# Weights converted ahead of a mask, a sigmoid under its own table, a last product in two banks, and outputs from another queue

## The chip, the cores and the metric

The kernel runs on one core of one Trainium2 chip. The core has a matrix engine (TensorE, PE in the profile), a vector engine (VectorE, DVE), an activation engine (ScalarE, ACT), GpSimd (POOL) and a sync engine (SP) that mainly issues transfers. Each engine takes its own instructions strictly in order, and the engines wait for one another through semaphores. Matmuls write to PSUM, which is divided into banks; DVE and ACT read the results from there. The metric is the device time of one execution in microseconds, lower is better; the profile shows one execution by itself.

## The reference

The first block is a gated linear recurrence over 768 tokens, for 4 batches and 8 heads of 48 channels. The second is a feed-forward block with a gate, of 384 to 1536 to 384 channels, over all 3072 tokens.

```python
f = 1.0 / (1.0 + np.exp(-f_logit))
for t in range(S):
    state = f[:, :, t, :, None] * state + k[:, :, t] (outer) v[:, :, t]
    y[:, :, t] = q[:, :, t] @ state
x = y.transpose(0, 2, 1, 3).reshape(B * S, H * D)
g = x @ w_gate
out = (g * sigmoid(g) * (x @ w_val)) @ w_out
```

Here "(outer)" stands for the outer product that the reference writes as an einsum. The three weight matrices come in 64-bit floats, everything else in 32-bit floats.

## The kernel before, in words

**Tiling.** The sequence is cut into six chunks of 128 tokens. A unit is one batch's part of one chunk, so chunk 0 holds units 0 to 3, chunk 1 units 4 to 7, and so on. The recurrence inside a chunk is done with products: `attention(u)` applies a sigmoid to the gates, multiplies them up in scans over time (`tails` at L549, `head` at L562), scales k and q with the results (`kT` at L559, `qT` at L568), multiplies the two into scores (`sc`, L586), masks the scores to the causal part (`A`, L596) and multiplies with v (`y`, L639, or L614 and L618). ACT then copies y into `xT` (L654), from which the feed-forward products of the chunk are made. The function is a generator: each `yield` ends a step, and the callers decide which other work goes between steps.

**Loads.** `load(u, what)` issues the transfers of f, k, q and v of a unit from SP. In chunks 0 and 1 f, k and q go to two rotating buffers each (`raw`), so a load has to wait until PE has transposed the unit two before.

**Weights.** [...]the weights come in pieces of 768 KB: `fetch` issues the transfer (L447) into one of four buffers, `sizes` has ACT make two tiles from a piece (`up` at L459, `top` at L461, each with two buffers), and `join` has DVE put them together in four kinds of steps (L467, L469, L471, L473), the last of which writes the weight. The first piece of the gate weights and the first of the value weights are converted in two halves each, so that the first product can start early; the lists `fetches`, `sizes` and `joins` hold what is still to be done, in order. A fetch has to wait until the piece four before has been read by both engines.

**Order.** The first part (chunk 0's recurrence, and the first steps of unit 4) is written out by hand around L1098 to L1157. At its end `in_order` makes PE, DVE and ACT keep the order in which the code was written. SP is not in that list, so a scheduler places its transfers. After that, `take_turns` mixes the feed-forward products of chunk 0 (`mlp_plain`: gate products at L712 with a silu on ACT at L724, value products with a multiply on DVE at L728, then the downward products at L737) with the recurrence of chunk 1, and with the rest of the weights.

**Tables.** ACT needs a table for sigmoid and another for silu, and loading one is an instruction of its own. Copies, absolute values and scalings work under either. In the first part ACT goes from silu back to the sigmoid of unit 4 (L535) and then to silu again.

**Chunks 1 to 5.** Their feed-forward block runs through `mlp_fifteen`, a scheme with fifteen block products instead of eighteen for each of the gate and the value, and then `down_seven`, seven block products instead of eight. Products go to PSUM banks from three pools: "A" (two banks), "B" (one) and "o" (two). ACT copies banks aside (`c` and `aside`, L892), and DVE adds and subtracts them (L786, L789). What DVE or the queues have to do after a product is put in `lagging` by `lag`, and written behind the next product. The outer loop takes the pieces of all chunks by due time and mixes in the recurrence of the chunk after.

**The end of a chunk.** In `down_seven`, `five` ends with the two additions for the upper output half `kept["o", 1]`, one of which reads the bank of `kept["p4"]`. `seven(0)` and `seven(1)` then make the last product, for two groups of 128 tokens. Both write the same bank, each half of it. After each, DVE adds it to `u5` into `kept["o", 0]`, and `put_out` (L997) issues the transfer of 192 KB to the output. All four output transfers of a chunk are issued from ACT's queue, except the very last of the kernel, which is issued from SP's. For chunks 1 to 4 DVE's eleven sums of tokens for the next chunk (`token_sums`, in L786 to L792) stand ahead of those two additions.

Of the kernel before, what the change touches and what calls it, by code (L numbers as in the profile page):

```python
# [12 lines left out]
AF = mybir.ActivationFunctionType  # L13
# [276 lines left out]
def short_path(ctx, tc, ident, least, judge, q, k, v, f_logit, moe_w_gate, moe_w_val, moe_w_out, out):  # L290
# [9 lines left out]
    nc = tc.nc  # L300
    B, H, S, D = q.shape
    C = 128
    NCH = S // C
    HP = H // 2
    W = 64
    DM = H * D
# [4 lines left out]
    N1 = C + 1  # L311
    NRAW = 2
# [24 lines left out]
    raw = {nm: [first_pool.tile([128, H, W], FP32, tag=f"{nm}raw{i}", name=f"{nm}raw{i}") for i in range(NRAW)]  # L337
           for nm in "qkf"}
# [23 lines left out]
    def pairs(t, off=0):  # L362
        return t[:, off:off + HP * N1].rearrange("p (a t) -> p a t", t=N1)
# [49 lines left out]
    def load(u, what="fkqv"):  # L413
        b, c = units[u]
        rows = slice(c * C, (c + 1) * C)
        for nm, src in (("f", f_logit), ("k", k), ("q", q), ("v", v)):
            if nm not in what:
                continue
            if nm == "v":
                dst = v_of(u)  # L420
            elif c < SQUARES:
                dst = raw[nm][u % NRAW]
            else:
                for n in range(4):
                    at = Q * (1 - n % 2)
                    nc.sync.dma_start(
                        out=rooms[nm][Q * n:Q * (n + 1), at:at + HP * RUN].rearrange("t (a e) -> t a e", a=HP),
                        in_=src[b, n // 2::2, rows, :].rearrange("a (t i) d -> t a (i d)", i=NI))
                continue
            nc.sync.dma_start(out=dst[:, :, 0:D], in_=src[b, :, rows, :].rearrange("h t d -> t h d"))  # L430
# [84 lines left out]
    def bank(name):  # L515
        return banks[-1].tile([128, 512], FP32, tag="a", name=name)

    def attention(u):
        b, c = units[u]
        fr, kr, qr = (raw[nm][u % NRAW] for nm in "fkq")  # L520
# [10 lines left out]
        if c >= SQUARES:  # L531
            nc.scalar.activation(squares("f"), squares("f"), AF.Sigmoid)
        else:
            p = transposed("fTp", fr)
            nc.scalar.activation(pairs(gate)[:, :, 1:N1], p, AF.Sigmoid)  # L535
        yield
        if c >= SQUARES:
            nc.vector.transpose(in_turn(pairs(gate)[:, :, 1:N1]), squares("f"))
# [145 lines left out]
    def in_order(since, engines):  # L684

        start = len(traced)
        while traced[start - 1] is not since:
            start -= 1
        for engine in engines:
            keep_order([ins for ins in traced[start:] if ins.engine == engine])  # L690
# [145 lines left out]
    def lag(f, *args):  # L836
        lagging.append(lambda: f(*args))  # L837
# [129 lines left out]
    def down_seven(c, h):  # L967

        DH = DM // 2
        s1 = [comb.tile([128, TH], FP32, tag=f"hs{j}", name=f"hs{j}") for j in range(NP)]
        b11, b12 = w_out[:, 0:NP, 0:DH], w_out[:, 0:NP, DH:DM]
        b21, b22 = w_out[:, NP:NF, 0:DH], w_out[:, NP:NF, DH:DM]
        kept = {}
        order = [*range(0, NP, 2), *range(1, NP, 2)]

        def hidden_sums(j):
            a11, a21, a12, a22 = (h[j][:, k, :] for k in range(4))
            plus(s1[j], a21, a22)  # L980
            minus(a21, a11, a21)

        def bank2(name, tag):
            pool = {"A": banks_a, "B": banks_b, "o": banks_o}[tag]
            return pool.tile([128, 512], FP32, tag=tag, name=name)[:, 0:DM].rearrange("p (n d) -> p n d", n=2)

        def add(p, lhsTs, rhs, first, part):
            for j in order[part * NP // 2:(part + 1) * NP // 2]:
                for n in range(2):
                    nc.tensor.matmul(p[:, n, :], lhsT=lhsTs[j][:, n * C:(n + 1) * C], rhs=rhs[:, j, :],  # L990
                                     start=first and j == order[0] and n == 0, stop=j == order[-1],
                                     skip_group_check=True)

        def of_h(k):
            return [h[j][:, k, :] for j in range(NP)]

        def put_out(half, n, queue):  # L997
            t0 = (2 * half + n) * S + c * C
            queue.dma_start(out=out[t0:t0 + C, :], in_=kept["o", half][:, n, :])

        def one(part):
            if part == 0:
                kept["o", 0], kept["o", 1] = out_rooms()
                kept["u"], kept["u5"] = (comb.tile([128, 2, TH], FP32, tag=t, name=t)[:, :, 0:DH]
                                         for t in ("c12", "c22"))
                kept["p"] = bank2("o11", "B")
            add(kept["p"], of_h(0), b11, True, part)
            if part:
                nc.scalar.copy(kept["u"], kept["p"])
                for j in order:  # L1010
                    lag(minus, h[j][:, 0, :], s1[j], h[j][:, 0, :])

        def two(part):
            add(kept["p"], of_h(2), b21, False, part)
            if part:
                nc.scalar.copy(kept["o", 0][:, :, 0:DH], kept["p"])
                for j in order:
                    lag(minus, h[j][:, 2, :], h[j][:, 2, :], h[j][:, 0, :])

        def three(part):  # L1020
            if part == 0:
                kept["p"] = bank2("o6", "A")
            add(kept["p"], of_h(0), down_sums[2], True, part)
            if part:
                lag(plus, kept["u"], kept["u"], kept["p"])

        def four(part):
            if part == 0:
                kept["p5"] = bank2("o5", "B")
            add(kept["p5"], s1, down_sums[1], True, part)  # L1030
            if part:
                lag(plus, kept["u5"], kept["u"], kept["p5"])

        def five(part):
            if part == 0:
                kept["p"] = bank2("o7", "o")
            add(kept["p"], of_h(1), b12, True, part)
            if part:
                lag(plus, kept["u"], kept["u"], kept["p"])
                lag(plus, kept["o", 1][:, :, DH:DM], kept["u"], kept["p5"])  # L1040
                lag(plus, kept["o", 1][:, :, 0:DH], kept["u"], kept["p4"])
                for n in range(2):
                    lag(put_out, 1, n, nc.scalar)

        def six(part):
            if part == 0:
                kept["p4"] = bank2("o4", "o")
            add(kept["p4"], of_h(3), down_sums[4], True, part)

        def seven(n):  # L1050
            if n == 0:
                kept["p"] = bank2("o3", "A")
            for j in order:
                nc.tensor.matmul(kept["p"][:, n, :], lhsT=h[j][:, 2, n * C:(n + 1) * C], rhs=b22[:, j, :],
                                 start=n == 0 and j == order[0], stop=j == order[-1], skip_group_check=True)
            lag(plus, kept["o", 0][:, n, DH:DM], kept["u5"][:, n, :], kept["p"][:, n, :])
            lag(put_out, 0, n, nc.sync if n and c == NCH - 1 else nc.scalar)

        return hidden_sums, [(DOWN / 2, lambda f=f, part=part: f(part))
                             for f in (one, six, two, three, four, five, seven) for part in range(2)]  # L1060
# [28 lines left out]
    def weights():  # L1089
        if fetches:  # L1090
            fetches.pop(0)()
        if sizes:
            sizes.pop(0)()
        if joins:
            joins.pop(0)()
# [10 lines left out]
    def run(b, *steps):  # L1106
        for s in steps:
            assert done[b] == s
            done[b] += 1
            for _ in range((3, 1, 4, 2, 3)[s]):  # L1110
                next(first[b])

    def load_ahead(u):

        if u + NRAW < B:
            load(u + NRAW, "fkq")
        load(u + 1, "v")
        fetches.pop(0)()
        if u + NRAW >= B:
            load(u + NRAW, "fkq")  # L1120

    run(0, 0, 1, 2)
# [1 line left out]
    for b in range(1, B):  # L1124
        if b == 1:
            run(1, 0)
            keep_warm(6)
        run(b, 1)
        run(b - 1, 3)
        run(b, 2)  # L1130
        load_ahead(b)
        if b + 1 < B:
            run(b + 1, 0)
        else:
            sizes.pop(0)()
        run(b - 1, 4)
    run(B - 1, 3)
    joins.pop(0)()
    run(B - 1, 4)

    hidden, last = mlp_plain(0)
    steps = attention_steps(1)
    for _ in range(2):
        sizes.pop(0)()
        joins.pop(0)()
    load(B + 1, "v")
    for _ in range(2):
        sizes.pop(0)()
    hidden[0]()
# [2 lines left out]
    joins.pop(0)()  # L1152
    hidden[1]()
    weights()
    hidden[2]()
    steps.pop(0)()
    in_order(mark, (mybir.EngineType.PE, mybir.EngineType.DVE, mybir.EngineType.Activation))  # L1157

# [135 lines left out]
```

## Time and profile before

The median of three runs is 622.11 us (620.12 to 622.82). The profiled execution has a span of 618.6 us.

| Engine | busy, us | share of the span |
|---|---|---|
| PE (matmul) | 599.7 | 97% |
| DVE | 500.3 | 81% |
| ACT | 293.5 | 47% |
| POOL | 5.0 | 1% |

By stage, from the busy times of each stretch:

| Stretch, us | what runs | PE busy | DVE busy | share of DMA engines in use |
|---|---|---|---|---|
| 0 to 31 | recurrence of chunk 0 | 24.70 of 31 | 25.81 | full |
| 31 to 62 | feed-forward of chunk 0 begins, weights arrive | 29.05 of 31 | 28.15 | full |
| 62 to 107 | its gate and value products | 45.00 of 45 | 42.58 | 0.58 |
| 148 to 245 | chunk 1 | 96.54 of 97 | 89.99 | 0.33 |
| 245 to 342 | chunk 2 | 96.14 of 97 | 80.45 | 0.28 |
| 608 to 618.6 | the last product and the outputs | 3.94 of 10.6 | 2.19 | 0.24 |

A busy PE need not be a PE at its peak, as matmuls are pipelined and their ends modelled. What counts for this change is where PE is not busy, and what ended those idle times. A weight load (PEld) runs beside the matmul ahead of it.

### The profile page before, as it was taken

What the parts mean: (1) busy time and instruction counts of PE and PEld (TensorE: products, weight loads), DVE (VectorE), ACT (ScalarE), POOL (GpSimd) and SP (SyncE); (2) the same over time, 40 slices, a digit from 0 to 9 for tenths busy, and PEclk for the clock granted to TensorE, in tenths of its full rate; (3) what the DMA queues carried; (4) which work ended last, traced back from release to release, by engine and by line L of the source; (5) the groups of instructions that cost most, each with busy time, mean ns of one, the idle gap of its engine ahead of it and who ended that gap; (6) DMA issues with size and microseconds to landing.
All of it is one profiled execution on the core that took longest, in us unless ns stands there. A gap on an engine that the chain in (4) does not pass through costs nothing.

```text
span 618.6 us, 10913 instructions
## 1 busy us (share of the span) xinstructions
PE 599.7 (97%) x4060; PEld 490.1 (79%) x4060; DVE 500.3 (81%) x961; ACT 293.5 (47%) x535; POOL 5.0 (1%) x27
## 2 busy tenths in 40 slices
PE   7898999999999999999999999999999999999995
PEld 4744545667888898888899788899888889888895
DVE  7889999878999978868897877987887985566741
ACT  2485645313875621557711557632367640366600
POOL 1000000000000000000000000000000000000000
PEclk9999999999999999999999999999999999999998
DMA  9999583005231324222224320323321300100001
GB/s 150 236 246 254 172 231 92 5 23 161 63 86 51 85 61 125 69 48 64 51 77 117 91 52 19 84 62 95 107 75 33 81 6 10 52 2 0 1 2 56
DMA packets 95678, 50.95 MB, mean 82 GB/s; under 512 B 56064, under 2 KB 89472, under 8 KB 95616
## 3 DMA queue, kind: packets, MB, share of 16 engines
q1 hardware_dynamic: 92304, 45.64, 30.5%
q10 hardware_dynamic: 3312, 4.52, 2.0%
q8 instruction: 34, 0.56, 0.4%
q14 instruction: 28, 0.23, 0.1%
HBM read 42.47 MB, written 4.72 MB: 76 GB/s over the span
## 4 chain that ended last, share of the span: by engine, by line
PE 77%; DVE 12%; ACT 4%; DMA 3%; issue 2%; SPq 1%; ACTq 0%; DVEq 0%
PE o L990 16%; PE A L887 15%; PE B L887 11%; PE o L737 5%; PE o L887 5%; PE c L887 5%; PE sc L586 4%; PE val L712 4%; PE gate L712 3%; PE y L618 2%; PE kt L590 2%; PE y L614 1%; PE dS L659 1%; DVE head L562 1%; DMA fraw<-in_f_logit_dram 1%
## 5 line engine op out<-in xcount | busy, mean ns | idle before, releaser
L887 PE MATMUL A<-xs,w_both 128*128 128x256 f32 x240 | 62.6, 383 | 3.5 <-ACT c L892 2.3
L990 PE MATMUL o<-w_out,h 128*128 128x192 f32 x360 | 62.1, 328 | 0.2 <-ACT aside L892 0.2
L990 PEld LDWEIGHTS o<-w_out,h 128*128 128x128 f32 x360 | 58.6, 190 | 0.8 <-ACT aside L892 0.4
L887 PEld LDWEIGHTS A<-xs,w_both 128*128 128x128 f32 x240 | 44.5, 190 | 12.4 <-ACT c L892 3.9
L892 ACT COPY c<-A 128x512 f32<-128x512 f32 x40 | 23.3, 583 | 65.1 <-DVE ob L786 33.9
L786 DVE TENSOR_TENSOR c<-c,aside 128x512 f32<-128x512 f32 x60 | 41.1, 686 | 14.8 <-ACT aside L892 13.8
L892 ACT COPY aside<-A 128x512 f32<-128x512 f32 x60 | 35.0, 583 | 33.0 <-PE A L887 33.0
L789 DVE TENSOR_TENSOR c<-c,aside 128x512 f32<-128x512 f32 x60 | 41.2, 687 | 7.3 <-ACT aside L892 7.3
L837 DVE TENSOR_TENSOR h<-h,c 128x256 f32<-128x256 f32 x100 | 41.2, 421 | 7.0 <-ACT h L903 6.7
L990 PE MATMUL o<-ws,h 128*128 128x192 f32 x240 | 41.7, 328 | 0.0
L887 PE MATMUL B<-xT,extra 128*128 128x256 f32 x160 | 41.4, 382 | 0.0
L887 PE MATMUL c<-xT,w_both 128*128 128x256 f32 x160 | 41.3, 381 | 0.0
L887 PE MATMUL A<-xs,extra 128*128 128x256 f32 x160 | 41.2, 380 | 0.0
L887 PE MATMUL B<-xs,w_both 128*128 128x256 f32 x160 | 41.1, 380 | 0.0
L903 ACT ACTIVATE h<-c 128x256 f32<-128x256 f32 x100 | 39.2, 415 | 3.0 <-DVE c L789 1.9
L892 ACT COPY aside<-B 128x512 f32<-128x512 f32 x60 | 34.9, 582 | 10.6 <-PE B L887 10.2
L990 PEld LDWEIGHTS o<-ws,h 128*128 128x128 f32 x240 | 39.2, 190 | 0.3 <-issue 0.2
L789 DVE TENSOR_TENSOR c<-o,c 128x512 f32<-128x512 f32 x40 | 27.5, 689 | 14.6 <-ACT h L903 9.5
L596 DVE TENSOR_TENSOR A<-sc,causal 128x512 f32<-128x512 f32 x48 | 30.6, 678 | 6.0 <-PE sc L586 6.0
L887 PEld LDWEIGHTS B<-xs,w_both 128*128 128x128 f32 x160 | 30.4, 190 | 4.1
L887 PEld LDWEIGHTS c<-xT,w_both 128*128 128x128 f32 x160 | 30.2, 190 | 4.3 <-DVE c L789 0.2
L887 PEld LDWEIGHTS A<-xs,extra 128*128 128x128 f32 x160 | 30.3, 190 | 4.1
(134 smaller groups left out, 1155.0 us busy)
## 6 DMA issues: line engine op xcount, KB each, us to landing
fsquares<-in_f_logit_dram SPq DMA_DIRECT2D x64, 96.0 KB, 2.3
ksquares<-in_k_dram SPq DMA_DIRECT2D x64, 96.0 KB, 2.3
qsquares<-in_q_dram SPq DMA_DIRECT2D x64, 96.0 KB, 2.3
v<-in_v_dram SPq DMA_DIRECT2D x24, 192.0 KB, 3.3
w<-in_moe_w_gate_dram SPq DMA_DIRECT2D x6, 768.0 KB, 6.1
w<-in_moe_w_val_dram SPq DMA_DIRECT2D x6, 768.0 KB, 5.6
w<-in_moe_w_out_dram SPq DMA_DIRECT2D x6, 768.0 KB, 5.3
out_dram<-ob ACTq DMA_DIRECT2D x23, 192.0 KB, 2.0
```

Of the source, the lines that this page charges most:

```text
L586: nc.tensor.matmul(sc[par][:, a * C:(a + 1) * C], lhsT=kT[r, a, :], rhs=qT[r, a, :], start=True, stop=True)
L590: nc.tensor.transpose(p[:, a * C:(a + 1) * C], kT[:, a, :], ident)
L596: nc.vector.tensor_tensor(A[:, par], sc[par].rearrange("p (a t) -> p a t", t=C), causal.unsqueeze(1).broadcast_to((128, HP, C)), ALU.mult)
L712: nc.tensor.matmul(p, lhsT=w[:, j, i, :], rhs=xT[c][:, i, :], start=(i == 0), stop=(i == KT - 1))
L737: nc.tensor.matmul(p, lhsT=h[n // 2][:, n % 2 * 2 + b // 2, b % 2 * C:(b % 2 + 1) * C], rhs=w_out[:, j, :], start=(n == 0), stop=(n == NF ...
L786: nc.vector.tensor_tensor(dst, a, b, ALU.add)
L789: nc.vector.tensor_tensor(dst, a, b, ALU.subtract)
L837: lagging.append(lambda: f(*args))
L887: nc.tensor.matmul(p[name][:, n, :], lhsT=weights_of[a][:, n, j, :], rhs=tokens[b], start=fresh and n == 0, stop=True, skip_group_check=True)
L892: nc.scalar.copy(t, p[name])
L903: nc.scalar.activation(dst, src[:, 0, :], AF.Silu)
L990: nc.tensor.matmul(p[:, n, :], lhsT=lhsTs[j][:, n * C:(n + 1) * C], rhs=rhs[:, j, :], start=first and j == order[0] and n == 0, stop=j == ...
```

## The change

The change has five edits, in three places.

1. **First weights before the mask.** The first half of the first gate piece is joined, and the first half of the value piece prepared, ahead of step 3 of the last unit of chunk 0, which holds its mask. The aim is that DVE does something useful while it waits for the scores.
2. **One sigmoid while its table is loaded.** A new function, `sigmoid_ahead`, applies the sigmoid to the raw gates of unit 4 before PE transposes them and before the first silu is due. After the transposition ACT only copies them. The aim is to spare the change to the sigmoid's table and back.
3. **Loads in written order.** f, k and q of unit 5 are no longer loaded from `load_ahead(3)`, but together with its v after the next weight piece has been fetched. SP joins the engines whose order is kept in this first part. For the transfers after it, the scheduler is still free: in the built program the v of unit 7 stands ahead of that weight piece.
4. **The last product in two banks.** `seven(0)` takes a bank from pool "A" and `seven(1)` one from pool "o", each as a product of its own. The bank that pool "o" gives is the one that `kept["p4"]` had.
5. **Outputs from SP's queue.** The two transfers of the lower output half are issued from SP for every chunk. The two of the upper half stay with ACT.

```diff
+    def sigmoid_ahead(u):
+        fr = raw["f"][u % NRAW]
+        nc.scalar.activation(fr, fr, AF.Sigmoid)
+        ahead.add(u)
...
-            nc.scalar.activation(pairs(gate)[:, :, 1:N1], p, AF.Sigmoid)
+            nc.scalar.activation(pairs(gate)[:, :, 1:N1], p, AF.Copy if u in ahead else AF.Sigmoid)
...
         def seven(n):
-            if n == 0:
-                kept["p"] = bank2("o3", "A")
+            p = bank2("o3", "Ao"[n])[:, n, :]
             for j in order:
-                nc.tensor.matmul(kept["p"][:, n, :], lhsT=h[j][:, 2, n * C:(n + 1) * C], rhs=b22[:, j, :],
-                                 start=n == 0 and j == order[0], stop=j == order[-1], skip_group_check=True)
-            lag(plus, kept["o", 0][:, n, DH:DM], kept["u5"][:, n, :], kept["p"][:, n, :])
-            lag(put_out, 0, n, nc.sync if n and c == NCH - 1 else nc.scalar)
+                nc.tensor.matmul(p, lhsT=h[j][:, 2, n * C:(n + 1) * C], rhs=b22[:, j, :], start=j == order[0],
+                                 stop=j == order[-1])
+            lag(plus, kept["o", 0][:, n, DH:DM], kept["u5"][:, n, :], p)
+            lag(put_out, 0, n, nc.sync)
...
-        if u + NRAW >= B:
+        if u + NRAW == B:
             load(u + NRAW, "fkq")
...
+    joins.pop(0)()
+    sizes.pop(0)()
     run(B - 1, 3)
+    sizes.pop(0)()
     joins.pop(0)()
     run(B - 1, 4)
...
-    for _ in range(2):
-        sizes.pop(0)()
-        joins.pop(0)()
-    load(B + 1, "v")
+    sigmoid_ahead(B)
+    joins.pop(0)()
     for _ in range(2):
         sizes.pop(0)()
...
     weights()
+    load(B + 1)
     hidden[2]()
     steps.pop(0)()
-    in_order(mark, (mybir.EngineType.PE, mybir.EngineType.DVE, mybir.EngineType.Activation))
+    in_order(mark, (mybir.EngineType.PE, mybir.EngineType.DVE, mybir.EngineType.Activation, mybir.EngineType.SP))
```

In the built program, three other things follow in the first part. The scores of unit 4 (`sc`) stand ahead of the third value product on PE rather than in the midst of it. On DVE, the first step (L467) of the third gate piece now stands ahead of the last step (L473) of the value piece before it, and so ahead of unit 4's scan (L549). And SP issues k, q and v of units 5 and 6 ahead of the third value piece.

More of the change, by code (lines that the diff above doesn't have):

```diff
@@ L516, in bank @@
         return banks[-1].tile([128, 512], FP32, tag="a", name=name)
+    ahead = set()
+    def sigmoid_ahead(u):
+        fr = raw["f"][u % NRAW]
+        nc.scalar.activation(fr, fr, AF.Sigmoid)
+        ahead.add(u)
     def attention(u):
```

## The prediction

> **What bounds the kernel now.** I began with the page's shares of the engines, then the waits of TensorE (PE) over the whole span, then the timeline at the places those waits name. PE is busy for 97% of the span, so the end moves only by what PE stands idle, plus what follows its last product.
>
> ```profile
> PE 599.7 (97%) x4060; PEld 490.1 (79%) x4060; DVE 500.3 (81%) x961; ACT 293.5 (47%) x535; POOL 5.0 (1%) x27
> ```
>
> PE's waits (engine, tile and line, who ended the wait, then total us, times, longest):
>
> ```profile
> PE sc L586 <- DVE qT L568: 3.3, 3, 1.8
> PE A L887 <- ACT c L892: 2.3, 4, 0.6
> ...
> PE fTp L527 <- DMA fraw<-in_f_logit_dram: 1.7, 3, 0.8
> PE gate L712 <- DVE w_both L473: 0.7, 1, 0.7
> ```
>
> Three concern the change: one wait of 1.8 us on `qT`, four of about 0.6 us on ScalarE (ACT) copies, and the first gate product's 0.7 us. From 60 to 150 us PE waits for nothing, so an early saving is carried through that stretch.
>
> The start of the first product, in the timeline (start, duration, engine, line; in brackets the idle time before it):
>
> ```profile
> 27.86 1.29 DVE L596 TENSOR_TENSOR A<-sc,causal 128x512 f32<-128x512 f32 x2 [1.25 <-PE sc L586]
> 29.07 0.35 DVE L467 TENSOR_SCALAR top<-top 128x384 f32<-128x384 f32 x1
> 29.93 0.48 ACT L654 COPY xT<-y 128x384 f32<-128x384 f32 x1 [0.83 <-PE y L639]
> 30.44 0.56 DVE L473 CUSTOM_DVE_ANT_0 w_both<-top,up 128x768 uint16<-128x768 uint16 x1
> ...
> 42.78 0.56 DVE L467 TENSOR_SCALAR top<-top 128x768 f32<-128x768 f32 x1 [1.59 <-ACT top L461]
> ```
>
> VectorE (DVE) idles 1.25 us before the mask of unit 3, then joins the first weights (L467 to L473, until 31.00); the gate starts at 31.14. At 42.78 DVE waits for ACT, which loads a table at 37.37, at 39.28 and at 42.76, 1.28 us each. The scan for unit 4 follows at 46.38, `qT` ends at 51.53, and PE's `sc` starts at 51.67 after the 1.81 us.
>
> The turn from one chunk to the next, and the end:
>
> ```profile
> 245.45 1.03 PE L887 MATMUL o<-xT,w_both 128*128 128x256 f32 x4
> 245.61 0.61 DVE L786 TENSOR_TENSOR ob<-c,o 128x192 f32<-128x192 f32 x2
> 246.03 0.34 ACTq L999 DMA_DIRECT2D out_dram<-ob  x1
> 246.41 0.58 ACT L892 COPY c<-A 128x512 f32<-128x512 f32 x1 [8.62 <-DVE ob L786]
> ...
> 607.87 4.07 PE L1054 MATMUL o<-w_out,h 128*128 128x192 f32 x24
> 611.98 0.62 DVE L786 TENSOR_TENSOR ob<-c,o 128x192 f32<-128x192 f32 x2 [2.29 <-PE o L1054]
> 612.66 0.38 SPq L999 DMA_DIRECT2D out_dram<-ob  x1
> ```
>
> `A` was ready at 244.75 (its product runs from 243.72 for 1.03), yet ACT copies it at 246.41: an output issue in ACT's own queue waits for DVE's `ob`. At the end both halves of `ob` wait for the whole last product.
>
> **What the Trainium skill says.** "ScalarE: Activation LUTs", section What ACT_TABLE_LOAD costs, gives some 1283 ns for a load and a drain of 1380 ns. The trace agrees on the load (1.28 us), but shows no such drain: a copy ends at 37.35, the load runs from 37.37, the silu starts at 38.66. I use 1.28. "PSUM — Partial Sum Buffer", section PSUM bank collisions raise a hardware error, asks for guarding by bank, not by address; the trace agrees, since the first half's add idles 2.29 us until the second half of the same bank is done. "DMA: Bandwidth & Descriptors", section Issuing engines are not separate DMA queues, says another issuing engine saves only sequencer time, usually small. Per issue it is (0.34 to 0.44 us); here the wait held in the queue is what counts.
>
> **The change part by part.** *First weights before the mask.* The join of half a piece takes 1.93 us (29.07 to 31.00). Moved behind `qT` (ends 26.55) it runs to about 28.5, filling the 1.25 us hole but pushing the mask from 27.86 to 28.42, by 0.56. Behind the mask come PE's `y`, then ACT's `xT`, which ended at 30.41 and now ends at 30.97. The gate needs both: before max(31.00, 30.41), after max(28.5, 30.97). Saving 0.03 us; I take 0.05. What is won is DVE time: it leaves the mask at 29.7 with one join done, 1.3 us ahead. ACT's earlier work on the second piece costs nothing: it landed at 25.6 and is wanted at 26.2.
>
> *One sigmoid while its table is loaded.* Added: one 128x512 activation, 0.60 us (row L535), put after `state` at about 31.4; its data landed at 30.8. Removed: two of the three loads, 2 x 1.28 us. Then, with the durations of the timeline. ACT: sigmoid to 32.0, half a piece (1.05) to 33.0, a wait to 33.4 for the buffer that the third half join frees, a whole piece (1.75) to 35.2, silu load to 36.5, silu to 37.1, gates copy to 37.65, second val piece (1.65) to 39.3. DVE: from 29.7 three half joins of 1.9 to 35.3, a whole join (3.1, from 37.38 to 40.5 before) to 38.35, a multiply to 38.95; the val piece's L467, L469 and both L471 from 39.35 to 41.6. There the new order puts the first step of the next gate piece (L467) ahead of the last step of this one and of the scan: ACT must have that piece, and it must have landed.
>
> *Loads in written order.* Before, that piece was issued at 38.97, behind five loads, and landed at 45.2. Now it follows the val piece and one `v`, and waits only for its buffer, which the third half join has read by about 32.9. The val piece landed at 36.3; a `v` took about 0.9 us and a piece 2.3 to 3.1 in the full stretch, so it lands at 39.5 to 40.3; I take 40.0. ACT finishes with it at 41.8. DVE: L467 to 42.35, L473 to 43.2, scan from 43.2. Before, scan to `qT` was 50.84 - 46.46 = 4.38; one 0.45 step is replaced by a 0.60 multiply, so `qT` starts at 47.75 and `sc` 0.83 later (51.67 - 50.84), at 48.6. PE gets there at 31.07 + (47.98 - 31.14) = 47.9, since `sc` now stands where val 2 stood. The wait is 0.65 instead of 1.81: **1.2 us** saved. Bounds: a landing by 39.8 leaves 0.45 (1.4 saved), one at 41.5 leaves 2.15 (0.3 lost). The next val piece lands some 3 us later than 48.4, near 51.5; its join ends near 57 and its product is due at 61.5, so this hides.
>
> *Outputs from SP.* ACT keeps two issues per chunk, whose data is ready at 241.66, and copies `A` at 244.75, while PE still runs B and o. So the wait goes. It is worth more than the 0.57 listed: the weight load, normally 0.86 after that at 245.24, came at 247.05, and the next at 247.80 rather than 246.96, so PE lost 0.84 us. Four turns: **3.4 us**. SP now waits for `ob`; behind it stand the next unit's `f` loads, which need a buffer read only after 249.56, while `ob` is done by 246.3.
>
> *Last product in two banks.* The second half takes the bank of `p4`, so PE waits for DVE's last read of it. That read ends at 241.63; the weight load was due at 241.61. With 0.06 to 0.14 us for the signal it comes 0.1 to 0.15 late, of which the turn above shows 0.11 absorbed (0.95 late, 0.84 lost). Five times 0 to 0.2 us; I take 0.05 each, 0.25 lost. At the end the first `ob` no longer waits, so the second ends 0.3 us sooner and so does SP's last issue. The last transfer's landing (3.9 us) is not the bound: SP's flag load and branch follow that issue, and its next event is at 616.7, after the 616.56 of the landing. So 0.3, not more.
>
> Sum: 0.05 + 1.2 + 3.4 - 0.25 + 0.3 = 4.7 us. 622.1 - 4.7 = **617.4 us**.
>
> **The rivals.** *Only one part pays* (the landing comes at 41 to 41.5 and the bank costs 0.2 each turn, or a turn finds a new limit in DVE). For it: DVE's read of `p4` and the load really coincide to 0.02 us. Against it: DVE waits for ACT after each turn (0.43 at 247.52), so it has room. With the early gain at zero: 622.1 - 3.4 + 1.0 - 0.3 = 619.4; with the turns halved instead: 622.1 - 1.2 - 1.7 + 0.25 - 0.3 = 619.1; with both, 620.3.
>
> *The early stage becomes the loss.* The DMA engines are full until 62 us, and SP now keeps to a written order in which a `v` waiting for PE stands ahead of the weights. If the gate piece lands at 46.5, ACT ends at 48.3, the scan starts at 49.7, `sc` at 55.1: a wait of 7.2, 5.4 worse than now. 622.1 + 5.4 - 3.4 + 0.25 - 0.3 = **624 us**. Against it: the piece is asked for 6 us earlier and with fewer bytes ahead.
>
> **How the numbers follow.** Forecast 0.62, one part alone 0.28, slower 0.10. The range goes from 615.5 (full table gain, no bank cost, and a base as at the lowest 620.1) to 620.3 (the first rival's end). Over 0.5% faster means below 619.0: nearly all of the forecast and a third of the first rival, 0.70; over 0.5% slower, most of the last, 0.07.
>
> **What would show it.** Right: one table load between 31 and 44 us; the third gate piece (the "next" one above) issued near 33 and landed near 40; `sc` waiting about 0.65 us; no PE wait on ACT's `c` at the four turns, and A copied about 1.7 us sooner; SP's last issue 0.3 us after DVE's add to a half. The gate still starts near 31.1. Wrong: a PE wait of over 0.2 us at the second half of the last product, a gate or val product waiting on L473 between 50 and 70 us, or DVE idle for long before its scan.

## The result and the profile after

The changed kernel takes 616.44 us (median of 4, 615.98 to 617.19), the kernel before 621.22 us beside it (620.12 to 622.82): a ratio of 0.9922, 95% interval 0.9894 to 0.995. The forecast was 617.4 from a base of 622.1, a saving of 4.7 us; measured between the medians were 4.8. The profiled spans are 614.2 and 618.6 us. One thing has to be known to read medians here: in some executions TensorE's granted clock is halved for 3.4 us, which costs up to 1.7 us, so the steps are read from traces, and from medians only where they differ by more.

To see where the 4.39 us between the two traces lie, take the start of the same product in both. Chunk 1's first product starts at 147.33 us before and 147.21 after: the early part of the change, forecast to bring 1.25 us, leaves 0.12. From one chunk's last product to the next chunk's the steps are 96.98, 96.92, 93.66 and 80.49 us before, and 96.08, 96.08, 92.81 and 79.64 after: 3.44 us in four turns. From the last product's end to the end of the span it is 6.63 before and 5.80 after: 0.83 us.

The shares of the engines in the page after:

```profile
PE 598.6 (97%) x4060; PEld 489.5 (80%) x4060; DVE 500.8 (82%) x961; ACT 291.5 (47%) x534; POOL 5.0 (1%) x27
```

TensorE's waits after (tile and line, who ended the wait, total us, times, longest):

```profile
PE fTp L536 <- DMA fraw<-in_f_logit_dram: 2.4, 2, 1.9
...
PE sc L595 <- DVE qT L577: 1.5, 2, 0.8
PE A L896 <- ACT aside L901: 1.3, 5, 0.3
...
PE o L746 <- DVE h L737: 0.4, 1, 0.4
```

The four waits of 0.6 us of A on ScalarE's `c` are gone, and the one of 1.8 us on `qT` too (the two left are earlier ones). New are 1.9 us on the forget gates of unit 3 (the fourth unit), 0.5 us on ScalarE's `state` at 15.8 us, and 0.4 us on an `h` at 108 us. The wait before `y` of unit 3 grew from 0.2 to 0.7 us, as the mask comes later, which the forecast had counted.

The first products and the table, in the timeline after:

```profile
28.97 0.56 DVE L473 CUSTOM_DVE_ANT_0 w_both<-top,up 128x768 uint16<-128x768 uint16 x1
29.45 1.28 DVE L605 TENSOR_TENSOR A<-sc,causal 128x512 f32<-128x512 f32 x2
...
31.51 0.48 ACT L663 COPY xT<-y 128x384 f32<-128x384 f32 x1 [0.42 <-PE y L648]
...
32.04 1.12 PE L721 MATMUL gate<-xT,w_both 128*128 128x512 f32 x2
...
36.26 1.28 ACT L733 ACT_TABLE_LOAD   x1
...
40.58 0.94 ACT L459 ACTIVATE up<-w 128x768 int32<-128x768 uint32 x1 [0.32 <-DMA w<-in_moe_w_gate_dram]
...
49.19 1.16 PE L595 MATMUL sc<-qT,kT 48*128 48x128 f32 x16
```

The first join stands ahead of the mask, which follows without an idle time. One table load stands where three were. The gate now waits only for `xT` (ready at 31.99), as forecast, but starts 0.9 us later than before, where it was to start at 31.1. The third gate piece was issued at 33.91 and landed at 40.48; ScalarE waited 0.32 us for it. `sc` has no bracket: TensorE did not wait, where 0.65 us were forecast. That is no gain over the forecast: `qT` was begun at 48.36 (forecast 47.75), and TensorE, whose gate had started late, came to `sc` only when `qT` was done.

A turn, and the end:

```profile
244.67 0.58 ACT L901 COPY c<-A 128x512 f32<-128x512 f32 x1 [7.00 <-PE A L896]
...
245.50 0.61 DVE L795 TENSOR_TENSOR ob<-c,o 128x192 f32<-128x192 f32 x2
245.87 0.85 SPq L1008 DMA_DIRECT2D out_dram<-ob  x2
...
246.19 1.03 PE L896 MATMUL A<-xs,w_both 128*128 128x256 f32 x4
...
604.31 4.06 PE L1062 MATMUL o<-w_out,h 128*128 128x192 f32 x24
606.47 0.35 DVE L795 TENSOR_TENSOR ob<-c,o 128x192 f32<-128x192 f32 x1 [0.34 <-PE o L1062]
606.88 2.25 SPq L1008 DMA_DIRECT2D out_dram<-ob  x2
608.41 0.35 DVE L795 TENSOR_TENSOR ob<-c,o 128x192 f32<-128x192 f32 x1 [1.59 <-PE o L1062]
```

ScalarE copies A when A is done (244.67) and not after DVE's `ob`; the output issues wait for `ob` in SP's queue (245.87), and the next A product has no wait in its bracket. At the end DVE adds the first half 1.94 us ahead of the second. All 24 weight loads of the last product run in 3.93 us without a break, so the bank taken from `p4` holds nothing up.

### The profile page after: what moved, and what is told of

Same layout as the page of the kernel before. It is cut to its first block, busy times and chain, and to the rows that moved or that the text cites. A ratio compares the mean times of both kernels' runs of the same rounds, so it can differ in the third digit from the quotient of the medians.

```text
span 614.2 us, 10901 instructions
## 1 busy us (share of the span) xinstructions
PE 598.6 (97%) x4060; PEld 489.5 (80%) x4060; DVE 500.8 (82%) x961; ACT 291.5 (47%) x534; POOL 5.0 (1%) x27
## 4 chain that ended last, share of the span: by engine, by line
PE 79%; ACT 4%; issue 2%; DVE 2%; ACTq 0%
PE o L999 19%; PE A L896 17%; PE B L896 13%; PE o L896 6%; PE c L896 5%; PE o L746 5%; PE o L1062 3%; PE sc L595 3%; PE y L627 2%; PE y L648 1%; PE kt L599 1%; PE y L623 1%; PE dS L668 1%; ACT L912 1%; ACT top L461 1%
## 5 line engine op out<-in xcount | busy, mean ns | idle before, releaser
L896 PEld LDWEIGHTS A<-xs,extra 128*128 128x128 f32 x160 | 30.3, 190 | 4.2
```

What stands on the lines that cost most here:

```text
L896: nc.tensor.matmul(p[name][:, n, :], lhsT=weights_of[a][:, n, j, :], rhs=tokens[b], start=fresh and n == 0, stop=True, skip_group_check=True)
```

## The experiments

Each ratio is to the kernel before, run beside it. In the first set it took 620.94 us, in the second 620.36, in the third 620.60.

### The four parts

**The queue alone**: before, with

```diff
-            lag(put_out, 0, n, nc.sync if n and c == NCH - 1 else nc.scalar)
+            lag(put_out, 0, n, nc.sync)
```

> The kernel before with the lower half's outputs issued from SP in every chunk, and nothing else (one bank, old early order). Queue theory: the four waits of PE on ACT's copy c go (0.86 us each by the two traces), so the span falls by about 3.4 us to 615.2; at the end both last outputs stand in SP's queue behind the whole product, so the tail stays near 6.6 us or grows by up to 0.3. Rival, bank theory (the turn is slow because the add of the first half waits for the whole bank): the four waits stay, span near 618.6.

617.71 us, ratio 0.9943 (0.9926 to 0.996). The waits on `c` are gone, and the steps between the last products are 96.18, 96.08, 92.82 and 79.64 us, as in the changed kernel. This is the main part: 3.2 us between the medians.

**The banks alone**: before, with the new `seven` but the old queues.

```diff
-            if n == 0:
-                kept["p"] = bank2("o3", "A")
+            p = bank2("o3", "Ao"[n])[:, n, :]
...
```

> The kernel before with the last product in two banks, and nothing else (outputs from ACT's queue as before). Queue theory: the four waits of 0.6 us on ACT's copy stay, since ACT still waits for DVE's ob behind the token sums; only the tail gets shorter, by 0.3 to 0.8 us: span 617.8 to 618.3. Bank theory: the waits go and the span falls to about 615. If the second half had to wait for the bank of p4, the last product would take over 3.93 us of weight loads; the trace of the changed kernel says it does not.

620.04 us, ratio 0.9985 (0.9975 to 0.9994). The steps between last products are 97.00, 96.93, 93.67 and 80.49 us, those of before to 0.02: the second bank costs nothing at a turn. The tail, from the last product's end to the end of the span, is 6.31 us: 0.3 us less than before in the trace, while the medians differ by 0.9. The span of this trace, 620.0 us, can't be held against the forecast 617.8 to 618.3, since its clock was halved from 52.6 to 56.0 us.

**The early part alone**: the changed kernel with the old `seven`, queues and banks.

> The kernel before with the early part alone (weights ahead of the mask, one sigmoid, loads in written order), old end of a chunk. Theory that DVE takes the gain back: the first gate product again starts near 32.0, PE is about 0.8 us ahead at 106, waits some 0.4 us for DVE's multiply at 108, and is 0.1 us ahead when chunk 1's first product starts at 147.2; span 618.4 to 618.6. Rival, an early gain is carried to the end: span 617.3 to 617.8.

621.06 us, ratio 0.9998 (0.9987 to 1.0009): nothing. Its waits tell why:

```profile
PE A L896 <- ACT c L901: 2.3, 4, 0.6
...
PE o L746 <- DVE h L737: 0.8, 1, 0.8
```

In this trace TensorE is 1.0 us ahead of the kernel before at the first down product (105.76 against 106.75) and then stands 0.8 us for DVE's `h`. Chunk 1's first product starts at 147.42, 0.09 later than before. The edits of the early part were not tried one by one, except for the order on SP below.

**The end alone**: before, with the new `seven`, both its banks and its queue.

> The kernel before with the queue and the banks together, old early part. Theory that DVE takes the early gain back: chunk 1's first product starts at 147.33 as before, four turns give 3.4 us and the tail 0.8: span 614.3, within 0.2 of the changed kernel's 614.2. Rival, the early part's gain lasts: span 615.0 to 615.5.

616.52 us, ratio 0.9918 (0.9903 to 0.9934): the whole effect of the change, without its early part. The trace missed the forecast span (616.7 us against 614.3), as its clock was halved from 53.3 to 56.7 us; its four steps are those of the changed kernel to 0.1 us.

### Where the early lead goes

In the changed kernel TensorE is 0.77 us ahead at 55.93 (the gate product that starts at 56.70 before) and still 0.77 at 105.98. Then:

```profile
107.74 0.68 DVE L737 TENSOR_TENSOR h<-h,val 128x512 f32<-128x512 f32 x1
108.47 0.91 PE L746 MATMUL o<-w_out,h 128*128 128x384 f32 x2 [0.40 <-DVE h L737]
```

The kernel before, at the same place:

```profile
106.75 2.74 PE L737 MATMUL o<-w_out,h 128*128 128x384 f32 x8
107.78 0.68 DVE L728 TENSOR_TENSOR h<-h,val 128x512 f32<-128x512 f32 x1
```

DVE makes that `h` 0.04 us sooner, whatever TensorE has gained. It had been up to 2 us ahead near 60 us, and lost it by 93.7, where both DVE streams fall into step; from 95 to 108 it is busy for 12.86 of 13 us in both. In the changed kernel DVE waits at 90.49 us for ScalarE:

```profile
88.74 0.93 ACT L459 ACTIVATE up<-w 128x768 int32<-128x768 uint32 x1 [3.58 <-DVE w_both L473]
...
90.49 0.56 DVE L467 TENSOR_SCALAR top<-top 128x768 f32<-128x768 f32 x1 [0.92 <-ACT top L461]
```

ScalarE had itself waited 3.58 us for DVE to free one of two `up` and `top` buffers. The next two kernels take that away: `up` goes straight into the weight's place, and the room gives `top` four buffers.

```diff
-            up = wst.tile(shape, I32, tag="up", name="up", bufs=NPART)
+            up = dst[:, part(m)].bitcast(I32)
...
-            top = wst.tile(shape, I32, tag="top", name="top", bufs=NPART)
+            top = wst.tile(shape, I32, tag="top", name="top", bufs=2 * NPART)
```

**More room in the changed kernel.**

> The changed kernel, but the rounded low words go straight into the weight's own place and the freed room gives four buffers instead of two to the other intermediate of a weight conversion, so ScalarE need not wait for VectorE before it prepares the next piece. Theory (the early lead of TensorE is lost at 108 us because VectorE, held up at 90.5 us by the two buffers, delivers the h of the first down products just in time): VectorE's idle times before a conversion (1.2 us at 82.7, 0.9 us at 90.5) vanish, TensorE's wait of 0.4 us for h at 108 us vanishes, chunk 1 starts 0.4 to 0.8 us earlier than in the changed kernel, and the time is 0.4 to 0.9 us under the whole change: 615.6 to 616.1 us beside 620.9 of before, ratio 0.991. Rival (TensorE itself, or the landing of the weights, sets the pace of that stretch): the idle times move elsewhere and the time is that of the whole change, 616.5.

617.07 us, ratio 0.9944 (0.993 to 0.9957). The trace answers as the theory said: DVE's waits for ScalarE from 31 to 110 us, 3.6 us in the changed kernel, are gone but for 0.2; there is no wait for `h` at 108 us, and DVE waits 1.56 us for TensorE there instead. The time does not: this execution began late (first gate product at 33.74 us, after a 2.2 us wait on the forget gates and a halved clock from 20.8 to 24.2 us), and the five times spread from 615.85 to 618.06. Inconclusive for the gain.

**More room in the kernel before.**

> The kernel before with the same edit of the conversion's buffers. Theory (before, TensorE came to the first down products with no lead, so it was its own bound there): no wait of TensorE is removed, and the time stays within 0.3 us of 620.9, although VectorE runs ahead. Rival (VectorE's conversions bind the stretch from 60 to 108 us in the kernel before as well): the time falls by 0.5 to 1.5 us.

621.67 us, ratio 1.0006 (0.9993 to 1.002): no change by the median. But it falls into two groups, five executions of 13 at 619.55 to 619.95, all below the lowest of before (620.13), the others at 621.2 and more with a lower mean granted clock. So the theory was too strict: some 0.5 us seem to be had in the kernel before as well, hidden by losses of clock in the other eight.

**The end with more room**: the end alone, with the edit of the buffers.

> The kernel before with the new end (two banks, outputs from SP's queue) and the roomier conversion buffers (low words straight into the weight's place, four buffers for the other intermediate), without the early part of the change. If the conversions' buffers bind the stretch up to 108 us, as the undisturbed runs of the kernel before with that edit said (619.6 against 620.3 us), the gains add: 0.5 to 1.0 us under the changed kernel run beside it, 615.3 to 615.9. If they don't, it equals it, 616.2 to 616.6.

616.16 us, ratio 0.9938 (0.9917 to 0.9958), beside 616.53 of the changed kernel run with it. In the trace, chunk 1 starts at 146.83, 0.50 us earlier than before, and at the first down products

```profile
106.44 2.74 PE L737 MATMUL o<-w_out,h 128*128 128x384 f32 x8
106.71 0.69 DVE L728 TENSOR_TENSOR h<-h,val 128x512 f32<-128x512 f32 x1 [1.56 <-PE val L712]
```

DVE waits for TensorE, not TensorE for DVE. The stretch from the first down product to chunk 1's first product sums it up over all traces: it takes 40.38 to 40.39 us in the four with more room, 40.57 to 40.80 in the seven without it in which TensorE came to the first down product at 106.75 or later, and 41.21 to 41.66 in the three in which it came sooner. So the buffers did hold the conversions up, and the lead of TensorE is given back there; the gain of this kernel is 0.5 us in this trace, 0.4 between medians, and less than the spread of the times. That lies between the two expectations, and it isn't shown to beat the changed kernel.

### The order of the loads

**Without the written order on SP**: the changed kernel with SP taken out of `in_order`.

```diff
-    in_order(mark, (mybir.EngineType.PE, mybir.EngineType.DVE, mybir.EngineType.Activation, mybir.EngineType.SP))
+    in_order(mark, (mybir.EngineType.PE, mybir.EngineType.DVE, mybir.EngineType.Activation))
```

> The changed kernel without the written order on SP's queue alone. The prediction's step of 1.2 us (third gate piece lands at 40 instead of 45 us): the piece lands late again, TensorE waits 1.8 us instead of 0.7 for qT before the scores of the fifth unit, and if that saving reached the end the time rises by about 1.2 us to 617.3 to 617.7. New theory (TensorE's lead is lost anyway at 108 us, where VectorE delivers h): the wait before the scores comes back, but the first products of chunk 1 start within 0.4 us of where they did, and the time stays within 0.4 us of the changed kernel run beside it.

618.79 us, ratio 0.9967 (0.9954 to 0.998): 2.3 us above the changed kernel beside it. The third gate piece was issued at 36.18 and landed at 41.76, 1.3 us later than in the changed kernel. ScalarE waits for it, DVE for ScalarE, and the scores for DVE:

```profile
41.87 0.90 ACT L459 ACTIVATE up<-w 128x768 int32<-128x768 uint32 x1 [2.84 <-DMA w<-in_moe_w_gate_dram]
43.58 0.56 DVE L467 TENSOR_SCALAR top<-top 128x768 f32<-128x768 f32 x1 [2.31 <-ACT top L461]
...
50.35 1.16 PE L595 MATMUL sc<-qT,kT 48*128 48x128 f32 x16 [2.50 <-DVE qT L577]
```

Chunk 1 starts at 147.71 in this trace, 0.50 later than in the changed one, near what the new theory said (0.4). The median is not explained by that: three of 15 executions take 616.39 to 616.67 us, within 0.6 us of the fastest of the changed kernel beside it (616.16), and the other 12 lie 0.9 to 3.7 us above 616.39, all with a lower granted clock. I had not expected this, and no trace of one of the 12 was kept.

**More room, and the loads free**: both edits.

> The changed kernel with the roomier conversion buffers and without the written order on SP's queue. Theory (the order puts the fourth unit's forget gates 1.1 us later in some executions, and VectorE no longer holds TensorE up at 108 us): gate products start at 31.2 us, no wait of TensorE for h at 108 us, time 615.2 to 616.0. Rival (nothing before 108 us matters): the time of the changed kernel run beside it.

620.77 us, ratio 0.9999 (0.9988 to 1.0009); both theories missed the time, though the gate started at 30.96 us and there was no wait for `h`. The third gate piece landed at 42.05. DVE waited 3.36 us for ScalarE's `top` of it, with 1.4 us more of the value piece's join than in the changed kernel between that wait and the scan. The wait for `qT` grew to 4.0 us, and no execution was under 619.5. By stretch (length; busy PE, PEld, DVE, ACT, POOL with counts; granted clock, DMA share, GB/s):

```profile
48.00:52.00 4.00, 0.02 (x2) 0.05 (x2) 4.00 (x10) 2.40 (x5) 0.00 (x0) 1.00 1.15 307
52.00:56.00 4.00, 4.00 (x22) 2.84 (x23) 3.93 (x8) 3.03 (x5) 0.00 (x0) 0.57 1.09 360
```

TensorE stands for nearly four microseconds, and then its clock is 0.57 of full speed for four: 1.7 us of its time, on top of the wait.

**The changed kernel again**, beside the last three.

> The changed kernel itself, beside the three others on one chip: 616.0 to 616.6 us, a ratio of 0.992 to 0.993. Its first gate product starts at 31.4 us in some executions and at 32.0 us or later in others, according to whether the fourth unit's forget gates land at 19.2 or at 20.4 us; TensorE waits 0.4 to 0.8 us for h at 108 us.

616.53 us, ratio 0.9934 (0.9917 to 0.9951). The fourth unit's forget gates landed at 20.34, the first gate product started at 33.10, and the clock was halved from 30.3 to 33.7. TensorE came to the first down product at 107.14, too late to wait for `h`, so the expected wait at 108 us is missing here.

### The end of the program

**A short last transfer**: the changed kernel, whose last output transfer carries 8 of its 128 rows; the other 120 rows of that tile are not written.

> The changed kernel whose very last output transfer carries 8 of its 128 rows; the other 120 rows of that tile are left out. Theory A (the end waits for the landing of the last output): the landing falls from 3.4 us to about 2.0 to 2.5 us after the issue and the tail after the last product from 5.8 to 4.4 to 5.0 us, time 615.1 to 615.7 us. Theory B, the prediction's (after the issue SP's flag load and branch set the end, and the landing is not the bound): the tail stays at 5.7 to 5.8 us, time 616.4.

616.39 us, ratio 0.9936 (0.9922 to 0.9949), tail 5.93 us. One sixteenth of the bytes, and a tail within those of the changed kernel's two traces (5.80 and 6.33): the landing of the last output is not what the end waits for.

**The left half of the columns ahead**:

```diff
...
+                for n in range(2 if c == NCH - 1 else 0):
+                    lag(put_out, 0, n, nc.sync, 0, DH)
...
-            lag(put_out, 0, n, nc.sync)
+            lag(put_out, 0, n, nc.sync, DH if c == NCH - 1 else 0)
```

> The changed kernel; in the last chunk the left half of the columns of the last two output tiles is sent from SP as soon as it is complete, some 20 us before the end, so the transfers behind the last two additions carry 96 KB each instead of 192 KB. Theory A (the landing is the bound): tail 5.2 to 5.6 us instead of 5.8, time 0.2 to 0.6 us under the whole change. Theory B (SP's sequence after the issue is the bound): tail 5.8 us, the same time. A third way: two more transfers in short pieces make SP or the queue later, and the time rises by up to 0.3 us.

616.88 us, ratio 0.994 (0.9926 to 0.9953), tail 6.00 us. The last transfer landed 2.8 us after its issue (3.4 in the changed kernel), and SP's next event came 0.8 us after the landing. Again no gain from a shorter transfer.

## Why the prediction was right, step by step

**Outputs from SP (3.4 us): right, mechanism and size.** The traces give 3.44 us over four turns, the queue alone 3.2 us between medians. Reading 0.84 us from the spacing of the weight loads rather than the listed wait of 0.57 made the size right: four times 0.57 would have been 2.3.

**"Two banks" (0.25 lost): the cost is zero.** DVE's read of `p4` ends 0.02 us after the weight load of the second half has begun, and neither that load nor the product breaks. The signal time of 0.06 to 0.14 us, taken from elsewhere in the trace, was not paid here. Perhaps only the product has to wait for the bank and not the weight load ahead of it; that isn't shown.

**The tail (0.3): the counted term is right, the tail gained more.** SP's last issue moved from 0.72 to 0.42 us after the last product, the forecast 0.3. The statement that the landing isn't the bound held in both experiments on it. In the traces of before and after alone it looked wrong, since SP's next event came 0.03 to 0.1 us after the landing in both; in four other traces it came before the landing, by up to 0.78 us. In that one, the banks alone, a later event of SP then stood some 0.3 us until a landing that took 4.47 us, so a late landing can still hold the end. The rest of the 0.83 us was not in the sum, and part of it is spread: over all traces the tail is 5.80 to 6.33 us in ten with two banks, both of these from the same changed kernel, and 6.44 to 6.63 in four with one. The means differ by 0.5 us. In three of these four, those in which ScalarE issues an output 0.24 us ahead of SP's last, some 0.2 of it is SP's flag load, the instruction behind that issue: 0.72 to 0.73 us there, 0.51 to 0.64 in all others. From SP's branch to its next event were 2.48 to 3.03 us, and what sets that stays open.

**First weights before the mask (gate at 31.1, 0.05 saved): not seen with the loads in written order.** With the whole early part but SP free, the gate started at 30.82 and 30.96 us, where six traces with the old early part have 31.11 to 31.40: a gain of some 0.3. With SP's order kept it started at 31.36 and 31.48 in two traces, in which unit 3's forget gates landed at 19.2 and 19.4 us, and at 32.04 to 33.74 in four, in which they landed at 20.3 to 20.5. In the two with SP free they landed at 19.1 and 19.3. All six with SP's order also have the wait of 0.5 us on `state` near 16 us, which the two without it lack. The order of those first loads is thus the likely cause, argued from eight traces and not tried by itself; the prediction had weighed the order only for the third gate piece and what follows it.

**One sigmoid and the loads in written order (1.2 us): the mechanism right, the size only in part.** The piece landed at 40.48 (forecast 40.0) and the scan began at 43.77 (43.2). With SP's order taken away the piece came at 41.76 and `sc` waited 2.50 us, near the forecast's bound of 2.15 for a landing at 41.5. What reached 56 us was a lead of 0.77 us and not 1.25, as TensorE had started its gate products 0.9 us late. Two readings in the sum were off by under 0.1 us: it took the scan from 46.46, where the timeline has 46.38, and the end of `qT` as 26.55, where the mask's line gives 26.61 (27.86 less its 1.25 of idle time).

**"From 60 to 150 us PE waits for nothing, so an early saving is carried through that stretch": this step failed**, and it took most of what was left of the 1.25 us of the early part. TensorE had no wait at 108 us because DVE's `h` came just in time: the multiply ended at 108.46, and the product that reads it, the seventh of eight from 106.75 at 0.33 us each, was due at 108.75. That is less than 0.3 us to spare, with DVE busy for 12.86 of the 13 us before. When TensorE came 0.77 us sooner, it waited 0.40 us, and at the next scores it was 0.11 us ahead of before (109.31 against 109.42): 0.66 us given back. "Perfetto Trace Analysis" in the Trainium skill, section Optimization Strategies, says to optimize what blocks the matmul engine when it stands idle; this case adds that an engine which never appears among the waits can be the next to block. The rival "only one part pays" described this part best, though it gave another reason.

By the forecast's own terms the traces show 0.1 us at the start instead of 1.25, 3.4 at the turns as forecast, 0 instead of 0.25 lost for the bank, and 0.8 instead of 0.3 at the end: 4.4 us against 4.7. The forecast came close because its large term was right and two errors went opposite ways, 1.15 us too much at the start, 0.8 too little at the bank and the end. That they cancel is luck. The agreement of the medians, 4.7 and 4.8, is luck in part too: the base of 622.1 is the middle of three executions of which two, at 622.11 and 622.82, lie in the upper of that kernel's two groups of times (last section). Beside 28 executions of the kernel before, the changed kernel run again saves 4.1 us.

## What to carry to other kernels

A transfer issued from a computing engine's queue holds up all that engine's work behind it until its data is ready: issue outputs from a queue with nothing to compute, and price the gain from the spacing of the waiting engine's weight loads. Before counting an early saving through a stretch without waits, look at the spare time of each operand there; an engine that is full and just in time gives the saving back. Shortening one long idle time of TensorE may be worth more than the wait itself, as the next section argues.

## What the runs showed of the hardware

- **The price of a TensorE idle time can be more than its length.** In seven of fourteen traces the granted clock fell to 0.5 for 3.41 us in the midst of the run, which takes 1.7 us of TensorE's time. Five of these came within 5 us of an idle time of 1.8 to 4.0 us, on `qT` near 50 us or on the forget gates near 19 us; in the other two a 2.0 us idle time lay ten microseconds back, with shorter ones between. "TensorE: Matmul & The Clock Gate" in the Trainium skill, section What's actually happening, describes such a half rate after an idle window of some 3.4 us, in a window that runs freely. The length and the half rate agree; the idle times here were mostly shorter than that window.
- **Where an idle time falls on these windows seems to decide.** The stretches of full clock ahead of the halved one last 13.65, 23.89, 44.37 or 47.79 us, which are 4, 7, 13 and 14 times 3.413. So the clock changes on a grid of 3.41 us, which lies differently in each execution. In the five traces with one long wait TensorE was busy for 17 to 47% of the grid window just ahead of the halved clock; in the kernel before, whose wait of 1.8 us was parted between two windows, no window from 7 us to the last product was under 53%, and its clock stayed full. The other two traces don't fit a limit of busy time alone: theirs had 54%, and an earlier window of 52 and 53% was followed by the full clock.
- The kernel before falls into two groups: 25 of 80 executions take 621.8 us or more, the other 55 between 620.07 and 621.13. Its one wait of 1.8 us and such a grid would make them so, which is argued, as its trace shows the full clock. How much of the 1.7 us reaches the end differs. With the old early part chunk 1 started 1.4 to 1.9 us later in two traces with the halved clock (148.98 and 149.23) than in two without (147.33 and 147.58). With the early part of the change it started at 147.72 and 147.97 in two with it, against 147.21 to 147.49 in three without: there a late TensorE doesn't wait for DVE's `h`.
- Writing `up` into the weight's own place cost nothing in DVE's L473 (0.95 to 0.97 us, 0.95 before) and freed a buffer for ScalarE.
- From the last output's issue to SP's next event were 3.47 to 4.01 us in twelve traces with 192 KB, 3.67 us with 96 KB and 3.59 with 12 KB, so at the end of a program the size of the last transfer made no difference here that shows beside the spread.
